# Attention and a mixture of experts on one core: sums kept in PSUM, low parts and softmax scaling between engines, reused w2 parts

## The chip, the cores and the metric

The kernel runs on one core of a Trainium2 chip. A core has TensorE (PE in the profile, with its weight loads as PEld), VectorE (DVE), ScalarE (ACT), GpSimd (POOL) and SyncE (SP, which here only issues DMAs). The metric is the device time of one execution in microseconds (us); lower is better.

## The reference

```python
def _attn_ref(q, k, v, n_global, n_local):            # 4 batches, 8 heads, 768 positions, head size 64
    scores = matmul(q, k^T) / sqrt(D)
    keep = (pos_k < n_global) | ((rel >= 0) & (rel < n_local))       # 8 and 96 here
    scores = where(keep, scores - slopes[h] * dist, -1e9)
    a = exp(scores - max(scores)); a = a / (sum(a) + 1e-9)
    return matmul(a, v)

def _moe_ref(x, domain_probs, w1, w2):                # x: 3072 x 512, 4 experts, 1024 hidden columns
    p = domain_probs / (domain_probs.sum(-1, keepdims=True) + 1e-9)
    for e in range(E):
        h = maximum(x @ w1[e], 0)
        out += p[:, e:e+1] * (h @ w2[e])
    return out
```

The attention's output, heads side by side, is the x of the mixture of experts. All is float32.

## The kernel before

**Precision.** A float32 matrix is split into a high part (a cast to fp32r, on ScalarE) and a low part (the float32 minus that cast). A product is three fp32r matmuls: high by high, low by high, high by low. Every operand of a matmul thus costs a cast and a subtraction; who does the subtraction is a choice between VectorE and GpSimd.

**Fewer products.** Each 2 x 2 block product of the experts is computed with seven block products in place of eight (a Winograd scheme). The weights enter as the sums A11, A12, S3, A22, S2, S1, S4 (`PAIRS1`, `PAIRS2` pack them in pairs), the activations as B11, B21, T3, T4, T2, T1, B22. For w1 the sums are made by `make_pair` in batch 0, written to DRAM by `keep`, and read back in batches 1 to 3. For w2, batch 0 uses plain block products on the raw halves, batch 1 uses the scheme and makes and keeps the sums, batches 2 and 3 read them.

**Units and chunks.** A batch is 16 units (4 experts x 4 groups of 256 hidden columns). `first(i)` is the w1 side of unit i: seven steps, each one product of six 128x384 matmuls. It uses three PSUM tiles: two called y and one z. A step's result is copied out by ScalarE (`part`), or added to such a copy on VectorE (`add`, into the SBUF tile h) and then multiplied by the mixture weight with a maximum against zero in one scalar_tensor_tensor (`weighed`). Two units make a chunk. `second(c)` is the w2 side of chunk c: in batch 0 sixteen steps, later fourteen, of six matmuls each. `hidden(k)` makes the operands of its k-th product: a block sum on VectorE where there is one, the cast on ScalarE, the low part. `collect` adds the PSUM result to the accumulators (`sums_lo` and `third` in the profile).

**Order.** The main loop emits a step of `first`, then a step of `second` for an older chunk (which may start `LAG` steps after its h is complete), and in between steps of the next batch's attention. At a batch's end `blocks` builds the seven operands from x, and six steps of `second` run alone (`ALONE`). In the start and for the first steps the written order is kept (`Ordered.on`); after that a scheduler orders each engine's queue by its own model of costs, and each queue is then executed in order.

**Attention.** `flow` is a pipeline over tiles of 128 queries. In one call a new tile gets its scores, the next older its exponentials, the one after that is scaled by the reciprocal of its sum, the oldest are transposed and weighed (`softmax`, `turn`, `weigh`). `prepare` transposes, splits and spreads queries and keys of a pair of heads in halves of 384 positions; `qd`, the spread query half, has one buffer.

**Buffers.** Weight pairs of w1 have three tiles (`w1p`), those of w2 four (`w2p`, two generations of two). A kept pair is written to DRAM by a DMA on GpSimd's queue as soon as it is made.

The profile gives nearly every instruction the line 42, that of the helper that records it, so rows are told apart by their tiles. Tile `hs` or `third` with reader `h` is an operand of `second`.

Of the kernel before, what the change touches and what calls it, by code (L numbers as in the profile page):

```python
# [185 lines left out]
def attn_moe_kernel(ctx: ExitStack, tc, q, k, v, n_global, n_local, domain_probs, w1, w2, out):  # L186
# [89 lines left out]
    class Pools:  # L276


        def __init__(self, stack, name, st, kd, qd, nat, natv, pb, pT, ps, pt, px):
            def sbuf(part, bufs):  # L280
# [142 lines left out]
    def softmax(A, new, old):  # L423
# [12 lines left out]
        for j in range(2):  # L436
            if new:
                ve.tensor_tensor_reduce(
                    new["pb"][:, j, pcol], ps[:, j, cols], nbias[:, 2 * pr + j, bcol],
                    1.0, 3.0e38, ALU.add, ALU.min, nmax[:, j : j + 1],  # L440
                )
                ac.activation(
                    new["pb"][:, j, pcol], new["pb"][:, j, pcol], AF.Exp, bias=nmax[:, j : j + 1], scale=-1.0,
                    accum_out=new["zsum"][:, j : j + 1],
                )
            if old:
                if j == 0:
                    ve.tensor_scalar_add(zsum, zsum, 1e-9)
                else:
                    ve.reciprocal(zsum, zsum)  # L450
        if old:
            for j in range(2):
                ve.tensor_scalar_mul(pb[:, j, old["pcol"]], pb[:, j, old["pcol"]], zsum[:, j : j + 1])

# [32 lines left out]
    def attention(b, A, early=False):  # L487
# [30 lines left out]
        def prepare(nat, got):  # L518
# [5 lines left out]
            prepare_k(A, nat["k", 0], 0, got)  # L524
            yield 1
            yield 1
            prepare_k(A, nat["k", 1], 1, got)
            yield 1
            nat["vg"] = windows(A, nat["v"])
            yield 1  # L530
            prepare_q(A, nat["q", 1], 1, got)
            yield 1
# [75 lines left out]
    def blocks(b, A, ks=(0, 1), low=po):  # L608
# [18 lines left out]
        yield 1  # L627
        split("B21", b21, low)
        ve.tensor_sub(b12, b22, b12)
# [30 lines left out]
    def split_pair(dst, src):  # L660
        ac.copy(dst[:, 0], src)
        po.tensor_tensor(dst[:, 1], src, f32(dst[:, 0]), op=ALU.subtract)

    def make_pair(dst, pair, q, sums):

        s2, s1 = sums[:, 0], sums[:, 1]
        if pair == ("A11", "A12"):
            po.tensor_add(s1, q[:, 0, 1], q[:, 1, 1])
            po.tensor_sub(s2, s1, q[:, 0, 0])
            split_pair(dst, q[:, :, 0])  # L670
            return
# [5 lines left out]
        if "S4" in pair:  # L677
            po.tensor_sub(q[:, 1, 0], q[:, 1, 0], s2)
        if pair == ("S3", "A22"):
            split_pair(dst, q[:, :, 1])  # L680
            return
        for n, a in enumerate(pair):
            k, m = {"S3": (0, 1), "S4": (1, 0), "A22": (1, 1)}[a]
            split_pair(dst[:, :, n : n + 1], q[:, k : k + 1, m])

    def keep(key, dst, shape):
        kept[key] = dp.tile(shape, F32R, name="kept_" + "_".join(str(n) for n in key))
        po.dma_start(f32(kept[key]), f32(dst))

# [6 lines left out]
    def pair_w1(j):  # L696
# [15 lines left out]
        make_pair(dst.rearrange("p s n (a f) -> p s n a f", a=2), PAIRS1[n], q, sums)  # L712
        keep((1, e, g, n), dst, shape)

# [20 lines left out]
    def next_w2():  # L735
# [6 lines left out]
        for u in range(2):  # L742
            _, e, g = units[2 * c + u]
            shape = [P, 2, 1 if b > 0 and n == 3 else 2, F4]
            dst = wts2[(c, n, u)] = w2p.tile(shape, F32R, name="w2p")
            if b == 0:
                split_pair(dst, raws2[(c, n, u)])
            elif b == 1:
                q = raws2[(c, u)].rearrange("p n (m f) -> p n m f", m=2)
                make_pair(dst, PAIRS2[n], q, sums2[(c, u)])  # L750
                keep((2, e, g, n), dst, shape)
            else:
                sy.dma_start(f32(dst), f32(kept[(2, e, g, n)]))

# [18 lines left out]
    def first(i):  # L773
# [7 lines left out]
        def product(dst, a, x, start=True):  # L781
            j, n = PLACE1[a]
            w = wts1[4 * i + j]
            m = 0
            for kt in range(2):
# [16 lines left out]

        def add(n, pm, other):
            ve.tensor_add(h[n], pm[:, :HALF], other)
            weighed(n, h[n])

# [5 lines left out]
        product(w, "A12", "B21")  # L812
        add("11", w, m1)
        yield
# [7 lines left out]
        product(y, "S3", "T3", start=False)  # L822
        add("22", y, other)
        yield
        product(z, "S4", "B22", start=False)
        add("12", z, part)
        yield
# [11 lines left out]
    def hidden(k):  # L839
# [12 lines left out]
        else:  # L852
            name = SCHEME[n][1]
            eng = ve if name in ("T4", "T1") else po
            if name == "T3":
# [30 lines left out]
    def multiply(pm, c, a, x, m, start, stop):  # L886

        n, u = a
        k = 0
        for kt in range(2):  # L890
# [22 lines left out]
    def second(c):  # L913
# [29 lines left out]
        for n, (a, _) in enumerate(SCHEME):  # L943
# [10 lines left out]
            if last:  # L954

                for eng, to, other in FINAL[n]:
                    eng.tensor_add(slot(b, to), slot(b, to), slot(b, other))
                if n == 5:
# [7 lines left out]
    with ExitStack() as start_stack:  # L966
        A = Pools(start_stack, "start", st=1, kd=2, qd=1, nat=2, natv=3, pb=4, pT=4, ps=3, pt=4, px=1)
        half = iter(())
# [25 lines left out]
    ps_mm = main.enter_context(tc.tile_pool(name="ps_mm", bufs=2, space=PSUM))  # L994
    A = Pools(main, "att", st=1, kd=1, qd=1, nat=3, natv=1, pb=2, pT=3, ps=1, pt=2, px=0)

    LAG, ALONE = 3, 6
    per = 7 * PER  # L1000
    count, span = NPAIR * (6 + NQT) + 5, per - 9
    firsts = (s for i in range(len(units)) for s in first(i))
    seconds = [second(c) for c in range(NCH)]
    xblocks = blocks(0, A, (1,))
    Ordered.on = True
# [4 lines left out]
    def step_second():  # L1010

        nonlocal chunk
        while chunk < NCH and state["done"] >= min(14 * (chunk + 1) + LAG, 7 * len(units)):
            if next(seconds[chunk], 0) is None:
                return True
            chunk += 1
# [84 lines left out]
```

## Time and profile before

| what | value |
|---|---|
| median of 2 runs | 1383.81 us (1383.67 to 1383.95) |
| the profiled execution | 1372.88 us, its span 1371.1 us |
| mean granted TensorE clock | 0.954 |
| PE busy | 1210.3 us (88%), 7201 matmuls |
| DVE busy | 988.5 us (72%), 1919 instructions |
| POOL busy | 664.6 us (48%), 624 instructions |
| ACT busy | 588.5 us (43%), 1271 instructions |
| DMA | 287.28 MB, mean 210 GB/s |

Busy time is the time in which an engine executed something. A stretch of the profile is given in us from the span's start. In a row of instructions the last part, after the second bar, is the idle time of the engine just before them and what ended it. In a row of waits the numbers are us in total, times, and the longest.

### The profile page before, as it was taken

What the parts mean: (1) busy time and instruction counts of PE and PEld (TensorE: products, weight loads), DVE (VectorE), ACT (ScalarE), POOL (GpSimd) and SP (SyncE); (2) the same over time, 40 slices, a digit from 0 to 9 for tenths busy, and PEclk for the clock granted to TensorE, in tenths of its full rate; (3) what the DMA queues carried; (4) which work ended last, traced back from release to release, by engine and by line L of the source; (5) the groups of instructions that cost most, each with busy time, mean ns of one, the idle gap of its engine ahead of it and who ended that gap; (6) DMA issues with size and microseconds to landing.
All of it is one profiled execution on the core that took longest, in us unless ns stands there. A gap on an engine that the chain in (4) does not pass through costs nothing.

```text
span 1371.1 us, 20747 instructions
## 1 busy us (share of the span) xinstructions
PE 1210.3 (88%) x7201; PEld 1148.8 (84%) x7201; DVE 988.5 (72%) x1919; ACT 588.5 (43%) x1271; POOL 664.6 (48%) x624
## 2 busy tenths in 40 slices
PE   6778899999979878879897788989999899999986
PEld 4657889999979778868786688989999799999985
DVE  7767777676766577867788796767787884666665
ACT  4745555455433444435343345444443325322322
POOL 5356666666753275566768742222232523333243
PEclk9989999999999988989998999999999999999999
DMA  7428766666455775757855767868776577777753
GB/s 146 140 71 236 222 193 191 184 210 209 150 165 179 221 227 188 237 195 246 250 200 168 238 195 242 267 201 262 238 253 209 200 250 253 263 256 257 251 202 115
DMA packets 188879, 287.28 MB, mean 210 GB/s; under 512 B 89856, under 2 KB 118624, under 8 KB 188768
## 3 DMA queue, kind: packets, MB, share of 16 engines
q1 hardware_dynamic: 168896, 220.87, 53.0%
q0 software_dynamic: 16384, 58.73, 11.3%
q10 hardware_dynamic: 3488, 6.29, 1.3%
q8 instruction: 59, 0.97, 0.3%
q14 instruction: 52, 0.43, 0.1%
HBM read 197.18 MB, written 65.06 MB: 191 GB/s over the span
## 4 chain that ended last, share of the span: by engine, by line
PE 54%; DVE 18%; DMA 11%; POOL 9%; issue 5%; ACT 4%; SPq 0%; ACTq 0%; DVEq 0%; POOLq 0%
PE pm L42 24%; PE y L42 16%; PE z L42 7%; DVE h L42 7%; PE pt L42 4%; DMA qd<-st_q 4%; POOL hs L42 3%; PE ps L42 3%; DVE pb L42 2%; POOL w2p L42 2%; DMA raw<-in_moe_w_dram 2%; DVE sums_lo L42 2%; DVE zsum L42 1%; DMA w2p<-kept 1%; ACT pb L42 1%
## 5 line engine op out<-in xcount | busy, mean ns | idle before, releaser
L42 PE MATMUL pm<-hs,w2p 128*128 128x384 f32 x2544 | 536.4, 346 | 63.1 <-DVE sums_lo L42 27.4
L42 PEld LDWEIGHTS pm<-hs,w2p 128*128 128x128 f32 x2544 | 459.4, 194 | 81.1 <-issue 17.7
L42 POOL TENSOR_TENSOR hs<-h,hs 128x768 fp32r<-128x768 f32 x120 | 225.6, 1881 | 409.0 <-ACT hs L42 372.8
L42 PE MATMUL y<-xT,w1p 128*128 128x384 f32 x1152 | 252.3, 353 | 23.9 <-DVE h L42 12.9
L42 ACT CAST hs<-h 128x768 fp32r<-128x768 f32 x190 | 158.6, 835 | 214.3 <-PE pm L42 185.7
L42 PEld LDWEIGHTS y<-xT,w1p 128*128 128x128 f32 x1152 | 209.4, 197 | 29.8 <-DVE h L42 14.5
L42 PE MATMUL y<-xB,w1p 128*128 128x384 f32 x768 | 164.8, 347 | 5.3 <-POOL w1p L42 2.5
L42 DVE SCALAR_TENSOR_TENSOR h<-h,mix 128x384 f32<-128x384 f32 x192 | 164.6, 857 | 3.9
L42 DVE TENSOR_TENSOR sums_lo<-pm,sums_lo 128x384 f32<-128x384 f32 x224 | 122.2, 550 | 52.4 <-PE pm L42 51.6
L42 DVE TENSOR_TENSOR h<-h,h 128x768 f32<-128x768 f32 x96 | 103.7, 1081 | 65.6 <-POOL hs L42 65.5
L42 PEld LDWEIGHTS y<-xB,w1p 128*128 128x128 f32 x768 | 135.4, 193 | 9.4 <-POOL w1p L42 3.1
L42 ACT ACTIVATE pb<-pb,nmax 128x256 f32<-128x256 f32 (+1 forms) x192 | 93.3, 487 | 110.3 <-DVE nmax L42 101.5
L42 DVE TENSOR_TENSOR h<-y,part 128x384 f32<-128x384 f32 x128 | 70.7, 552 | 96.0 <-POOL hs L42 43.7
L42 ACT COPY part<-y 128x384 f32<-128x384 f32 x128 | 61.3, 479 | 116.4 <-PE y L42 109.0
L42 DVE TENSOR_SCALAR pb<-pb,zsum 128x256 f32<-128x256 f32 (+1 forms) x192 | 102.3, 568 | 2.9
L42 DVE CUSTOM_DVE_ANT_0 pb<-ps,nbias 128x256 f32<-128x256 f32 (+1 forms) x192 | 71.9, 394 | 38.5 <-PE ps L42 34.6
L42 DVE TENSOR_TENSOR hs<-h,hs 128x768 fp32r<-128x768 f32 x70 | 87.0, 1242 | 13.2 <-ACT hs L42 11.7
L42 DVE TENSOR_TENSOR third<-pm,third 128x384 f32<-128x384 f32 x126 | 68.4, 550 | 32.2 <-PE pm L42 32.1
L42 PE MATMUL z<-xB,w1p 128*128 128x384 f32 x384 | 82.6, 349 | 0.0
L42 PE MATMUL z<-xT,w1p 128*128 128x384 f32 x384 | 81.2, 344 | 1.1 <-ACT xT L42 1.1
L42 PE MATMUL ps<-kd,qd 128*128 128x256 f32 x288 | 54.8, 307 | 28.8 <-DMA qd<-st_q 25.2
L42 POOL TENSOR_TENSOR w2p<-raw,w2p 128x512 fp32r<-128x512 f32 (+1 forms) x48 | 56.2, 1177 | 45.7 <-ACT w2p L42 45.2
(121 smaller groups left out, 1646.5 us busy)
## 6 DMA issues: line engine op xcount, KB each, us to landing
w1p<-kept SPq DMA_DIRECT2D x144, 512.0 KB, 4.5
w2p<-kept SPq DMA_DIRECT2D x96, 512.0 KB, 5.1
kept<-w1p POOLq DMA_DIRECT2D x48, 512.0 KB, 3.7
kept<-w2p POOLq DMA_DIRECT2D x48, 512.0 KB, 4.0
qd<-st_q SPq DMA_DIRECT2D x96, 192.0 KB, 5.1
raw<-in_moe_w_dram SPq DMA_DIRECT2D x32, 512.0 KB, 5.7
w1p<-kept SPq DMA_DIRECT2D x48, 256.0 KB, 3.2
half<-in_moe_w_dram SPq DMA_DIRECT2D x32, 256.0 KB, 3.1
```

The lines of the kernel that those rows point to most:

```text
L42: ins = fn(*args, **kwargs)
```

## The change

- In `first`, the sums of "11", "22" and "12" are written to PSUM (to the bank of "11" for "22", in place for the others) and `weighed` reads them there.
- In `hidden`, in batch 1 all low parts but that of "11" are made by VectorE; in batches 2 and 3 all but those of "11" and "22". Before, VectorE made two of seven. Two low parts of `blocks`, and all the last batch's final sums, go to VectorE too.
- In the attention of batches 1 to 3 ScalarE multiplies the exponentials by the reciprocal; in all batches ScalarE adds the 1e-9.
- Of w2, batch 0 keeps A11, A12 and A22, and batch 1 reads them; it makes S3, S2, S1 and S4.
- `keep` no longer writes at once on GpSimd's queue: the write is noted, and issued on SP's queue when the first product that uses the pair is emitted.
- The second query half is prepared three preparation steps earlier, and `LAG` is 4 in place of 3, one more for the first chunk.

```diff
...
                 )
             if old:
                 if j == 0:
-                    ve.tensor_scalar_add(zsum, zsum, 1e-9)
+                    ac.activation(zsum, zsum, AF.Copy, bias=1e-9)
                 else:
                     ve.reciprocal(zsum, zsum)
         if old:
             for j in range(2):
-                ve.tensor_scalar_mul(pb[:, j, old["pcol"]], pb[:, j, old["pcol"]], zsum[:, j : j + 1])
+                p = pb[:, j, old["pcol"]]
+                if A.scale == "vector":
+                    ve.tensor_scalar_mul(p, p, zsum[:, j : j + 1])
+                else:
+                    ac.activation(p, p, AF.Copy, scale=zsum[:, j : j + 1])
 
     def turn(A, tile_):
 
...
             yield 1
             prepare_k(A, nat["k", 0], 0, got)
             yield 1
+            prepare_q(A, nat["q", 1], 1, got)
             yield 1
             prepare_k(A, nat["k", 1], 1, got)
             yield 1
             nat["vg"] = windows(A, nat["v"])
             yield 1
-            prepare_q(A, nat["q", 1], 1, got)
             yield 1
 
         def prepare_all(pr):
...
 
         split("B11", b11, ve)
         yield 1
-        split("B21", b21, low)
+        split("B21", b21, ve)
         ve.tensor_sub(b12, b22, b12)
         yield 1
         ve.tensor_add(b11, b12, b11)
...
         ac.copy(dst[:, 0], src)
         po.tensor_tensor(dst[:, 1], src, f32(dst[:, 0]), op=ALU.subtract)
 
+    def make_sums(q, sums):
+        po.tensor_add(sums[:, 1], q[:, 0, 1], q[:, 1, 1])
+        po.tensor_sub(sums[:, 0], sums[:, 1], q[:, 0, 0])
+
     def make_pair(dst, pair, q, sums):
 
-        s2, s1 = sums[:, 0], sums[:, 1]
         if pair == ("A11", "A12"):
-            po.tensor_add(s1, q[:, 0, 1], q[:, 1, 1])
-            po.tensor_sub(s2, s1, q[:, 0, 0])
+            make_sums(q, sums)
             split_pair(dst, q[:, :, 0])
             return
         if pair == ("S2", "S1"):
...
         if "S3" in pair:
             po.tensor_sub(q[:, 0, 1], q[:, 0, 0], q[:, 0, 1])
         if "S4" in pair:
-            po.tensor_sub(q[:, 1, 0], q[:, 1, 0], s2)
-        if pair == ("S3", "A22"):
-            split_pair(dst, q[:, :, 1])
-            return
+            po.tensor_sub(q[:, 1, 0], q[:, 1, 0], sums[:, 0])
         for n, a in enumerate(pair):
             k, m = {"S3": (0, 1), "S4": (1, 0), "A22": (1, 1)}[a]
             split_pair(dst[:, :, n : n + 1], q[:, k : k + 1, m])
 
-    def keep(key, dst, shape):
-        kept[key] = dp.tile(shape, F32R, name="kept_" + "_".join(str(n) for n in key))
-        po.dma_start(f32(kept[key]), f32(dst))
+
+    waiting = {}
+
+    def keep(pair):
+        for key, src, shape in waiting.pop(pair, ()):
+            kept[key] = dp.tile(shape, F32R, name="kept_" + "_".join(str(n) for n in key))
+            sy.dma_start(f32(kept[key]), f32(src))
 
     def load_w1(i):
         if i < PER:
...
         q = raws1[i].rearrange("p (n a) (m f) -> p n m a f", n=2, m=2)
 
         make_pair(dst.rearrange("p s n (a f) -> p s n a f", a=2), PAIRS1[n], q, sums)
-        keep((1, e, g, n), dst, shape)
+        waiting[(1, j)] = [((1, e, g, n), dst, shape)]
 
 
     seq2 = [(c, n) for c in range(NCH) for n in (range(2) if c < CPB else range(4))]
...
             shape = [P, 2, 1 if b > 0 and n == 3 else 2, F4]
             dst = wts2[(c, n, u)] = w2p.tile(shape, F32R, name="w2p")
             if b == 0:
+
                 split_pair(dst, raws2[(c, n, u)])
-            elif b == 1:
-                q = raws2[(c, u)].rearrange("p n (m f) -> p n m f", m=2)
-                make_pair(dst, PAIRS2[n], q, sums2[(c, u)])
-                keep((2, e, g, n), dst, shape)
-            else:
-                sy.dma_start(f32(dst), f32(kept[(2, e, g, n)]))
+                waiting.setdefault((2, c, n), []).append(
+                    ((2, e, g, n), dst, shape) if n == 0 else ((2, e, g, 4), dst[:, :, 1:], [P, 2, 1, F4])
+                )
+                continue
+            one = dst[:, :, :1]
+            if n == 0 or b > 1:
+                sy.dma_start(f32(one if n == 1 else dst), f32(kept[(2, e, g, n)]))
+            if n == 1:
+                sy.dma_start(f32(dst[:, :, 1:]), f32(kept[(2, e, g, 4)]))
+            if b > 1:
+                continue
+            q, sums = raws2[(c, u)].rearrange("p n (m f) -> p n m f", m=2), sums2[(c, u)]
+            if n == 0:
+                make_sums(q, sums)
+                continue
+            make_pair(one if n == 1 else dst, (("S3",), ("S2", "S1"), ("S4",))[n - 1], q, sums)
+            waiting.setdefault((2, c, n), []).append(
+                ((2, e, g, n), one if n == 1 else dst, [P, 2, 2 if n == 2 else 1, F4])
+            )
 
         if made2[0] < len(seq2):
             c1, n1 = seq2[made2[0]]
...
         def product(dst, a, x, start=True):
             j, n = PLACE1[a]
             w = wts1[4 * i + j]
+            keep((1, 4 * i + j))
             m = 0
             for kt in range(2):
                 for wi, xi in ((0, 0), (1, 0), (0, 1)):
...
             ac.copy(dst, src[:, :HALF])
             return dst
 
-        def add(n, pm, other):
-            ve.tensor_add(h[n], pm[:, :HALF], other)
-            weighed(n, h[n])
+        def add(n, to, pm, other):
+            ve.tensor_add(to[:, :HALF], pm[:, :HALF], other)
+            weighed(n, to[:, :HALF])
 
         y = ps_h.tile([P, 512], F32, name=f"y{i % 2}")
         product(y, "A11", "B11")
...
         yield
         w = ps_h.tile([P, 512], F32, name=f"y{1 - i % 2}")
         product(w, "A12", "B21")
-        add("11", w, m1)
+        add("11", w, w, m1)
         yield
         product(y, "S2", "T2", start=False)
         part = copy(y)
...
         other = copy(z)
         yield
         product(y, "S3", "T3", start=False)
-        add("22", y, other)
+        add("22", w, y, other)
         yield
         product(z, "S4", "B22", start=False)
-        add("12", z, part)
+        add("12", z, z, part)
         yield
         product(y, "A22", "T4", start=False)
         weighed("21", y[:, :HALF])
...
             src, eng = h[PLAIN[n]], ve
         else:
             name = SCHEME[n][1]
-            eng = ve if name in ("T4", "T1") else po
+            eng = po if name == "11" or name == "22" and c >= 2 * CPB else ve
             if name == "T3":
                 ve.tensor_sub(h["12"], h["22"], h["12"])
             elif name == "T4":
...
     def multiply(pm, c, a, x, m, start, stop):
 
         n, u = a
+        keep((2, c, n))
         k = 0
         for kt in range(2):
             w = wts2[(c, n, kt)]
...
             if last:
 
                 for eng, to, other in FINAL[n]:
+                    eng = ve if b == B - 1 else eng
                     eng.tensor_add(slot(b, to), slot(b, to), slot(b, other))
                 if n == 5:
                     yield from output(b, 0, 1, 3)
...
     mp = main.enter_context(tc.tile_pool(name="mp", bufs=3))
     Ordered.on = True
     with ExitStack() as start_stack:
-        A = Pools(start_stack, "start", st=1, kd=2, qd=1, nat=2, natv=3, pb=4, pT=4, ps=3, pt=4, px=1)
+        A = Pools(start_stack, "start", st=1, kd=2, qd=1, nat=2, natv=3, pb=4, pT=4, ps=3, pt=4, px=1, scale="vector")
         half = iter(())
         mix = mixture(A)
         for n, _ in enumerate(attention(0, A, early=True)):
...
     tp2 = main.enter_context(tc.tile_pool(name="third", bufs=1))
     ps_h = main.enter_context(tc.tile_pool(name="ps_h", bufs=1, space=PSUM))
     ps_mm = main.enter_context(tc.tile_pool(name="ps_mm", bufs=2, space=PSUM))
-    A = Pools(main, "att", st=1, kd=1, qd=1, nat=3, natv=1, pb=2, pT=3, ps=1, pt=2, px=0)
-
-
-
-    LAG, ALONE = 3, 6
+    A = Pools(main, "att", st=1, kd=1, qd=1, nat=3, natv=1, pb=2, pT=3, ps=1, pt=2, px=0, scale="scalar")
+
+
+
+    LAG, ALONE = 4, 6
     per = 7 * PER
     count, span = NPAIR * (6 + NQT) + 5, per - 9
     firsts = (s for i in range(len(units)) for s in first(i))
     seconds = [second(c) for c in range(NCH)]
-    xblocks = blocks(0, A, (1,))
+    xblocks = blocks(0, A, (1,), ve)
     Ordered.on = True
     next(xblocks)
     next(xblocks)
...
     def step_second():
 
         nonlocal chunk
-        while chunk < NCH and state["done"] >= min(14 * (chunk + 1) + LAG, 7 * len(units)):
+        while chunk < NCH and state["done"] >= min(14 * (chunk + 1) + LAG + (chunk == 0), 7 * len(units)):
             if next(seconds[chunk], 0) is None:
                 return True
             chunk += 1
```

The pools of the start are made with `scale="vector"`, those of the other batches with `scale="scalar"`.

More of the change, by code (lines that the diff above doesn't have):

```diff
@@ L276, in attn_moe_kernel, with __init__ @@
     class Pools:
-        def __init__(self, stack, name, st, kd, qd, nat, natv, pb, pT, ps, pt, px):
+        def __init__(self, stack, name, st, kd, qd, nat, natv, pb, pT, ps, pt, px, scale):
+            self.scale = scale
             def sbuf(part, bufs):
```

## The prediction

> **What bounds the kernel now.** I first read the busy shares and the forty slices of the page, then cut the span where a batch's first w1 product starts (75, 401, 760 and 1065 us) and where the last w1 product ends (1322 us), and asked for the busy time of each stretch.
>
> ```profile
> PE 1210.3 (88%) x7201; PEld 1148.8 (84%) x7201; DVE 988.5 (72%) x1919; ACT 588.5 (43%) x1271; POOL 664.6 (48%) x624
> 75.00:401.00 326.00, 292.84 (x1799) 279.63 (x1799) 234.19 (x434) 163.24 (x370) 217.70 (x245) 0.97 0.60 187
> 401.00:760.00 359.00, 303.57 (x1737) 289.64 (x1738) 262.78 (x463) 153.29 (x330) 206.84 (x200) 0.90 0.66 212
> 760.00:1065.00 305.00, 280.33 (x1720) 267.16 (x1719) 231.21 (x476) 130.51 (x285) 103.62 (x73) 0.97 0.74 233
> 1065.00:1322.00 257.00, 247.32 (x1401) 243.11 (x1400) 174.29 (x277) 84.10 (x132) 86.68 (x46) 0.99 0.71 244
> 1322.00:1371.00 49.00, 33.80 (x173) 28.86 (x171) 28.65 (x41) 11.76 (x16) 17.56 (x9) 0.95 0.38 136
> 1150.00:1300.00 150.00, 149.43 (x861) 148.85 (x860) 97.16 (x167) 48.07 (x75) 47.87 (x26) 1.00 0.75 257
> ```
>
> The columns are stretch, length, then busy us (and count) of PE, PEld, DVE, ACT and POOL, the granted TensorE clock, DMA share and GB/s. The share of 88% on PE is an average over unlike stages. The last row is what a PE-bound stage looks like: 149.4 of 150 us busy, 861 matmuls, 0.174 us each, clock 1.00. Batches 1 and 2 (rows 3 and 4) run the same matmuls (1737 and 1720), yet batch 1 needs 359 us and batch 2 only 305. What differs is POOL: 207 us against 104, since batch 1 also builds the w2 combinations. DVE is busier too, 263 against 231 us for the same list of instructions, and the clock is 0.90 against 0.97. So in batch 1 PE is not the bound. What ends its waits, and what DVE spends, is in the next rows, all of 401 to 760 us.
>
> ```profile
> PE pm L42 <- DVE sums_lo L42: 19.4, 7, 5.5
> PE y L42 <- DVE h L42: 12.9, 4, 5.7
> DVE h L42 <- POOL hs L42: 28.8, 10, 8.0
> L42 DVE SCALAR_TENSOR_TENSOR h<-h,mix 128x384 f32<-128x384 f32 x48 | 49.5, 1032 | 0.9
> L42 DVE SCALAR_TENSOR_TENSOR h<-y,mix 128x384 f32<-128x384 f32 x16 | 8.7, 547 | 0.6 <-PE y L42 0.6
> L42 DVE TENSOR_TENSOR h<-h,h 128x768 f32<-128x768 f32 x27 | 34.4, 1276 | 5.6 <-POOL hs L42 5.6
> L42 DVE TENSOR_SCALAR pb<-pb,zsum 128x256 f32<-128x256 f32 (+1 forms) x48 | 33.8, 740 | 0.7
> L42 DVE TENSOR_SCALAR zsum<-zsum 128x2 f32<-128x2 f32 x24 | 12.6, 525 | 8.7 <-ACT pb L42 8.7
> L42 DVE TENSOR_TENSOR hs<-h,hs 128x768 fp32r<-128x768 f32 x14 | 19.1, 1364 | 0.3 <-ACT hs L42 0.2
> L42 POOL TENSOR_TENSOR hs<-h,hs 128x768 fp32r<-128x768 f32 x34 | 64.1, 1887 | 48.0 <-ACT hs L42 47.8
> L42 POOL DMA_DIRECT2D kept<-w2p x54 | 30.2, 560 | 7.1 <-POOL w2p L42 4.2 <-issue 2.4 <-PE y L42 0.3
> L42 POOL TENSOR_TENSOR w2p<-raw,w2p 128x512 fp32r<-128x512 f32 (+1 forms) x40 | 48.1, 1210 | 42.1 <-ACT w2p L42 41.7
> ```
>
> PE waits mostly for DVE, and DVE waits 28.8 us for POOL's low parts. The two scalar_tensor_tensor rows do the same arithmetic on the same 128x384: from PSUM it takes 547 ns, from SBUF 1032. The scaling (740 ns) and even an add on two columns (525 ns) are far above their size. One stretch shows why.
>
> ```profile
> 602.76 0.36 DVE L42 TENSOR_SCALAR pb<-pb,zsum 128x256 f32<-128x256 f32 x1
> 602.91 0.57 POOL L42 DMA_DIRECT2D kept<-w2p  x1
> 603.04 6.31 DVE L42 SCALAR_TENSOR_TENSOR h<-h,mix 128x384 f32<-128x384 f32 x1
> 603.51 1.30 POOL L42 TENSOR_TENSOR w2p<-raw,w2p 128x512 fp32r<-128x512 f32 x1
> 604.76 1.81 POOL L42 TENSOR_TENSOR hs<-h,hs 128x768 fp32r<-128x768 f32 x1
> 607.12 1.81 POOL L42 TENSOR_TENSOR hs<-h,hs 128x768 fp32r<-128x768 f32 x1
> 609.97 2.26 PE L42 MATMUL pm<-hs,w2p 128*128 128x384 f32 x6 [4.32 <-DVE sums_lo L42]
> ```
>
> An instruction of half a microsecond stands for 6.31 us while POOL works without a gap, and PE then idles 4.32 us for the accumulation queued behind it. A DVE instruction on SBUF operands is slowed by a busy POOL. The PSUM form is not: 547 ns beside the busiest POOL.
>
> **The change, part by part.** All terms are us of the profiled execution (1372.88, span 1371.1).
>
> *PSUM outputs.* Three adds per unit now write PSUM and the weighing reads PSUM. No row has a DVE write to PSUM. The nearest, a DVE read from it, differs from the SBUF form by 0.14 us at the least (687 against 547, below), so I bound the add's cost by 0.14 either way, 7 per batch, and take zero. The weighing goes from 1032 to 547: batch 1 gains 48 x 0.485 = 23.3. The other batches:
>
> ```profile
> L42 DVE SCALAR_TENSOR_TENSOR h<-h,mix 128x384 f32<-128x384 f32 x48 | 48.3, 1007 | 1.3
> L42 DVE SCALAR_TENSOR_TENSOR h<-h,mix 128x384 f32<-128x384 f32 x46 | 33.9, 737 | 0.8
> L42 DVE SCALAR_TENSOR_TENSOR h<-h,mix 128x384 f32<-128x384 f32 x51 | 35.0, 687 | 0.9
> ```
>
> Batches 0, 2, 3 in order: 22, 9 and 7. [...]
>
> The add's sum now stays in a bank: "22" is put where "11" was, two products before the next unit starts in that bank. DVE must be under two products (4.2 us) late. The bank of "21" already allows it only one, and with it PE waits 12.9 us on `h` in batch 1, so I cost the new wait at nothing; without that cover each microsecond of lateness is 16 us per batch.
>
> *Softmax on ScalarE.* DVE loses 33.8 and 12.6 in batch 1. ACT gains 48 instructions. The nearest rows are these, of the whole run:
>
> ```profile
> L42 ACT ACTIVATE pb<-pb,nmax 128x256 f32<-128x256 f32 x160 | 80.6, 505 | 87.0 <-DVE nmax L42 81.1 <-DVE zsum L42 5.7
> L42 ACT CAST w1p<-raw 128x256 fp32r<-128x256 f32 x48 | 18.2, 405 | 23.4 <-PE y L42 12.1 <-POOL raw L42 8.4 <-POOL w1p L42 1.1
> L42 ACT ACTIVATION_READ_ACCUMULATOR pb<-pb,nmax 128x1 f32 x192 | 36.1, 188 | 0.0
> ```
>
> Bounds 0.405 and 0.505; with a per-partition scale I take the second, 24 us, plus 24 x 0.19 = 5 for the small add. ACT goes from 153 to some 180 of 300 us, beside everything. Behind the new ACT instructions stand the evacuations and casts; the transposes that use the scaled tile come a whole softmax step later, which covers half a microsecond. [...]
>
> *Low parts.* In batch 1 four of seven move from POOL to DVE per chunk, 32 in all; three in batches 2 and 3, 24 each. Bounds: 0.95 undisturbed (the 954 below, same size) and 1.364 as now. POOL will still be some 40% busy; I take 1.15, so +36.8 in batch 1. A moved low part also waits for its ACT cast; the accumulations and weighings queue behind it. The 14 already there waited 0.3 in total. In return DVE no longer waits for POOL before overwriting a block, -28.8, and its block sums fall from 1276 to batch 2's 1068, 27 x 0.21 = -5.6.
>
> ```profile
> L42 DVE TENSOR_TENSOR h<-h,h 128x768 f32<-128x768 f32 x31 | 33.1, 1068 | 21.8 <-POOL hs L42 21.8
> L42 DVE TENSOR_TENSOR h<-h,h 128x768 f32<-128x768 f32 x38 | 36.3, 954 | 38.2 <-POOL hs L42 38.1
> L42 DVE TENSOR_SCALAR pb<-pb,zsum 128x256 f32<-128x256 f32 (+1 forms) x48 | 23.8, 530 | 0.6
> PE ps L42 <- DMA qd<-st_q: 25.2, 9, 4.5
> L42 POOL TENSOR_TENSOR w1p<-sums,w1p 128x512 fp32r<-128x512 f32 x16 | 20.9, 1306 | 14.9 <-ACT w1p L42 14.8
> L42 ACT CAST w1p<-sums 128x512 fp32r<-128x512 f32 x16 | 9.9, 616 | 23.0 <-issue 13.1 <-POOL sums L42 4.4 <-POOL raw L42 2.1
> kept<-w1p POOLq DMA_DIRECT2D x48, 512.0 KB, 3.7
> w2p<-kept SPq DMA_DIRECT2D x96, 512.0 KB, 5.1
> ```
>
> *Reuse of w2, and the kept writes on SP.* POOL loses in batch 1 the 32 low parts (60), its DMA issues (30) and the A11, A12 and A22 splits (some 35): from 207 to about 80. The reused parts come back by DMAs issued two generations ahead; 5.1 us each, hidden as in batch 2, which reads all weights so at DMA share 0.74. The 128 kept writes now stand in SP's queue ahead of q, k, w1 and qd transfers, and are issued only when TensorE first uses the pair. A pair is rewritten three or more products before its use; a product of six matmuls alternates with six of w2, 12 x 0.174 = 2.1, so 6.2 us; the landing of 3.7 lies beside the pair's own second product. I cost it at nothing; the second rival prices it.
>
> *Query halves, LAG, last sums.* The second query half is transposed three preparation steps earlier. Its buffer is single, so the transfer still waits for the third tile's scores, and only the transposing and splitting leave the 25.2 us wait: I take a third, 8 over three batches, inside the sums below. One more step of lag gives low parts 2 us more; no cost, since PE's list is unchanged.
>
> **The sum.** *Batch 1:* DVE's queue -23.3 - 33.8 - 12.6 + 36.8 - 5.6 - 28.8 = -67, which would give 292. PE cannot go much below batch 2's 280 busy, and I let batch 1 reach batch 2's present 305: -54 (bounds -20, if a third of the relief arrives, and -80, PE nearly dense). *Batch 2:* DVE -9 - 24 - 8 + 25 = -16, with half of 22 of POOL waits and a share of qd, but PE idles only 25 of 305: -10 (0 to -22). *Batch 0:* weighing, scaling and issue relief all fall on a stage with 33 idle: -15 (0 to -30). *Batch 3 and tail:* PE has 10 idle of 257; the tail idles 15 of 49 and its lows go from 1.89 to 0.95: -6 (+4 to -15). Start: 0. Together -85: 1372.9 - 85 = 1288. The median of the runs, 1383.81, is 0.8% above the profiled 1372.88; on that scale 1298.
>
> **Rivals.**
> 1. *DVE becomes the bound.* It takes over 80 instructions. If low parts stay at 1.364 and each waits for its ACT cast as long as it does now for POOL, batch 1 gets back 7 + 29 of its 67 and loses some more in PE's coupling: -20, other batches -12 in all: 1341, or 1351 on the scale of the median. For it: DVE is already 73% busy in batch 1, its one cover an idle POOL. Against it: batch 2 runs at 76% with PE at 92%. 0.17.
> 2. *Slower: the kept writes hold their pairs.* A w1 pair cannot be refilled before its write has landed. If SP is stuck behind another wait when TensorE takes up a pair, the write comes late, cast and low part after it, and PE waits. The chain is 3.7 landing + 0.6 cast + 1.3 low part = 5.6 of 6.2 us; so it bites from 0.6 us of SP lateness. If each of batch 0's 64 pairs costs 2 us, +128: 1372.9 - 85 + 128 = 1416, 1427 on the median's scale. For it: SP's queue is in order. Against: many pairs have four or five products, and SP only issues. 0.05.
> 3. *Within 2%.* The scheduler reorders around the new costs; what DVE gains is lost to qd, ACT and clock waits, and about 15 remain: 1358, 1369. 0.08.
>
> **How the numbers follow.** The forecast holds 0.70. Its own bounds are -42 to -130 with terms that don't all end together; the 80% range runs from 1255 (-128 before scaling) to 1350, which takes in most of the first rival. A change under 2% (1356 to 1411) is what I take a measurement of this kernel as unable to tell from none: faster 0.87, same 0.08, slower 0.05.
>
> **What would show it.** After: `h` weighing entirely from PSUM near 550 ns; the wait of DVE for POOL's low parts gone in batch 1; POOL near 80 us there; low parts on DVE near 1.1 us; batch 1's clock at 0.96 or more and its length near 300. Wrong if DVE is over 90% busy in batch 1, if PE's waits name `kept` DMAs or ACT's `w1p`, or if PE waits at a unit's first product for "22".

## The result

The changed kernel takes 1285.81 us (median of 1281.94 and 1289.68) against 1383.81 before: ratio 0.929, 95% interval 0.917 to 0.941. Run again later beside the other versions, it took 1281.99 against 1372.26: 0.935, interval 0.930 to 0.940. The median of one and the same kernel differs by about 1% between sessions (for the kernel before 1383.81, 1369.98, 1369.29 and 1372.26 us), so what follows compares ratios to the kernel before of the same session. The profiled execution took 1281.94 (span 1280.1) against 1372.88.

First the stages of these two profiled executions, again as busy time of stretches (length, then busy us and counts of PE, PEld, DVE, ACT, POOL, the clock, DMA share, GB/s). This time the cuts are where a batch's first w1 matmul stands by count (672 to a batch). By that count batch 2 ends at 1081 before, not at the 1065 of the prediction, so the rows of before are given for these cuts too; the kernel before, then the changed one:

```profile
80.00:392.00 312.00, 285.49 (x1750) 273.43 (x1750) 228.15 (x424) 158.18 (x359) 210.89 (x242) 0.97 0.62 192
392.00:755.00 363.00, 303.95 (x1742) 290.05 (x1741) 262.20 (x462) 153.66 (x331) 212.00 (x202) 0.90 0.65 208
755.00:1081.00 326.00, 294.29 (x1781) 280.24 (x1780) 250.02 (x496) 138.87 (x296) 112.55 (x79) 0.96 0.73 231
1081.00:1324.00 243.00, 237.93 (x1364) 234.31 (x1365) 162.48 (x265) 77.88 (x123) 79.40 (x42) 1.00 0.73 250
```

```profile
85.00:391.00 306.00, 288.11 (x1753) 273.77 (x1752) 166.50 (x356) 177.84 (x431) 172.78 (x179) 0.98 0.74 237
391.00:692.00 301.00, 279.13 (x1731) 268.12 (x1729) 204.99 (x411) 163.78 (x388) 104.29 (x103) 0.97 0.81 252
692.00:988.00 296.00, 282.53 (x1779) 271.23 (x1778) 225.29 (x448) 158.91 (x364) 57.94 (x41) 1.00 0.81 253
988.00:1234.00 246.00, 239.97 (x1369) 234.64 (x1368) 186.00 (x296) 80.05 (x126) 35.27 (x19) 1.00 0.73 248
1234.00:1280.00 46.00, 32.01 (x169) 26.83 (x168) 31.77 (x46) 11.81 (x17) 5.52 (x3) 0.98 0.45 150
```

Batch 1 is 62 us shorter, batch 2 30, batch 0 6; batch 3 is 3 longer, the start 5 longer. The stages of a second profiled execution of the changed kernel lie within about 2 us of these. Of batch 1's 62 us, TensorE's idle time gave 37 (59 to 22) and its busy time for the same matmuls 25 (304 to 279), while the granted clock went from 0.90 to 0.97; no run here separates the clock from the idle time. Batch 1 now runs like batch 2, with POOL at a half. The rows that answer to those of before, from 391 to 692 us of the changed kernel (groups, then waits):

```profile
L42 DVE SCALAR_TENSOR_TENSOR h<-y,mix 128x384 f32<-128x384 f32 x47 | 25.9, 552 | 1.2 <-PE y L42 0.5
L42 DVE TENSOR_TENSOR y<-y,part 128x384 f32<-128x384 f32 x32 | 17.9, 560 | 15.4 <-PE y L42 11.6 <-PE pm L42 1.8 <-issue 1.0
L42 DVE TENSOR_TENSOR hs<-h,hs 128x768 fp32r<-128x768 f32 x39 | 42.8, 1098 | 21.7 <-ACT hs L42 21.7
L42 DVE TENSOR_TENSOR h<-h,h 128x768 f32<-128x768 f32 x26 | 28.1, 1081 | 20.9 <-POOL hs L42 20.7
L42 ACT ACTIVATE pb<-pb,zsum 128x256 f32<-128x256 f32 (+1 forms) x48 | 21.2, 487 | 15.2 <-DVE zsum L42 15.2
L42 ACT ACTIVATE zsum<-zsum 128x2 f32<-128x2 f32 x24 | 4.9, 204 | 0.5
```

```profile
PE y L42 <- ACT part L42: 9.9, 3, 7.3
PE ps L42 <- DVE nmax L42: 5.0, 1, 5.0
PE pm L42 <- DMA w2p<-kept: 3.6, 4, 1.4
```

The add costs the same into PSUM (560 ns) as it did into SBUF (552), the weighing 552, scaling on ScalarE 487. PE's 19.4 us of waits for the accumulations and 12.9 for h no longer stand in the list.

### The profile page after: what moved, and what is told of

Its sections match the earlier page's. It is cut to its first block, busy times and chain, and to the rows that moved or that the text cites. A ratio compares the mean times of both kernels' runs of the same rounds, so it can differ in the third digit from the quotient of the medians.

```text
span 1280.1 us, 20773 instructions
## 1 busy us (share of the span) xinstructions
PE 1179.6 (92%) x7201; PEld 1117.9 (87%) x7201; DVE 871.8 (68%) x1768; ACT 642.9 (50%) x1495; POOL 405.1 (32%) x391
## 4 chain that ended last, share of the span: by engine, by line
PE 47%; DMA 11%; DVE 4%; ACT 2%; POOL 2%; issue 2%; SPq 1%; ACTq 0%; DVEq 0%; POOLq 0%
PE pm L42 23%; PE y L42 13%; DMA w2p<-kept 7%; PE z L42 7%; PE pt L42 3%; DMA out_dram<-hs 2%; PE ps L42 1%; ACT hs L42 1%; DVE h L42 1%; DMA raw<-in_moe_w_dram 1%; POOL hs L42 1%; SPq L42 1%; DVE third L42 1%; DVE hs L42 1%; DMA kept<-w2p 1%
## 5 line engine op out<-in xcount | busy, mean ns | idle before, releaser
L42 PE MATMUL pm<-hs,w2p 128*128 128x384 f32 x2544 | 518.3, 338 | 27.1 <-DMA w2p<-kept 13.8
L42 PEld LDWEIGHTS pm<-hs,w2p 128*128 128x128 f32 x2544 | 445.0, 188 | 43.5 <-issue 13.9
L42 PEld LDWEIGHTS y<-xT,w1p 128*128 128x128 f32 x1152 | 201.6, 191 | 28.8 <-ACT part L42 13.5
L42 POOL TENSOR_TENSOR hs<-h,hs 128x768 fp32r<-128x768 f32 x40 | 74.1, 1853 | 418.9 <-ACT hs L42 351.2
L42 DVE TENSOR_TENSOR hs<-h,hs 128x768 fp32r<-128x768 f32 x150 | 158.9, 1060 | 59.5 <-ACT hs L42 58.7
L42 DVE SCALAR_TENSOR_TENSOR h<-y,mix 128x384 f32<-128x384 f32 x192 | 105.8, 552 | 20.0 <-POOL hs L42 15.5
L42 DVE TENSOR_TENSOR y<-y,part 128x384 f32<-128x384 f32 x128 | 71.7, 561 | 58.3 <-PE y L42 43.0
L42 POOL TENSOR_TENSOR w1p<-raw,w1p 128x512 fp32r<-128x512 f32 (+1 forms) x64 | 58.9, 934 | 81.4 <-ACT w1p L42 77.9
L42 ACT ACTIVATE pb<-pb,zsum 128x256 f32<-128x256 f32 (+1 forms) x144 | 64.6, 487 | 30.7 <-DVE zsum L42 30.7
L42 PE MATMUL pt<-ident,pb 128*128 128x128 f32 x352 | 58.7, 281 | 14.9 <-DVE pb L42 13.1
```

Of the source, the lines that this page charges most:

```text
L42: ins = fn(*args, **kwargs)
```

## The experiments

I split the change into five parts, ran four of them alone, and ran the changed kernel with each of the five taken out. *Theory 1*, the prediction's: the gain is VectorE's time, given back because its instructions are fewer and not stretched by GpSimd. *Theory 2*: GpSimd's queue was the brake, and what it delays, TensorE and VectorE wait for. The two do not exclude each other: a loaded GpSimd may stand behind both VectorE's 28.8 us of waits for its low parts and the weighings of 1042 ns from SBUF, 547 from PSUM, in batch 1 before.

### One part alone

Sums in PSUM:

```diff
-        def add(n, pm, other):
-            ve.tensor_add(h[n], pm[:, :HALF], other)
-            weighed(n, h[n])
+        def add(n, to, pm, other):
+            ve.tensor_add(to[:, :HALF], pm[:, :HALF], other)
+            weighed(n, to[:, :HALF])
```

> The kernel before with one part of the change: the sums of 11, 22 and 12 stay in PSUM. If VectorE's time is what was gained (theory 1), the weighing falls from 857 to about 550 ns and VectorE loses some 60 us of busy time, half of it in batch 1; PE's waits for h and the sums shrink, and the time falls by 25 to 35 us, to about 1353. If GpSimd's queue was the brake (theory 2), VectorE goes on waiting for GpSimd's low parts and the time falls by under 10. If TensorE's new waits for the held banks bite, PE's waits at y name DVE and the time does not fall.

Measured: 1356.12 against 1369.98, ratio 0.988 (0.981 to 0.996). Faster by 14, half of what theory 1 gave it, though the weighing now reads PSUM, where it takes 552 ns in the changed kernel for 1042 before. Its batch 1, and the scaling there:

```profile
389.00:739.00 350.00, 294.49 (x1743) 280.73 (x1742) 255.66 (x465) 153.40 (x331) 211.24 (x202) 0.93 0.69 216
L42 DVE TENSOR_SCALAR pb<-pb,zsum 128x256 f32<-128x256 f32 (+1 forms) x48 | 38.7, 836 | 0.7
```

The weighing alone was worth 23 us of VectorE's time in this stage, but its busy time fell by 7 (262 to 256): other instructions took longer, the scaling among them, 836 ns instead of 740.

Scaling on ScalarE:

```diff
-                    ve.tensor_scalar_add(zsum, zsum, 1e-9)
+                    ac.activation(zsum, zsum, AF.Copy, bias=1e-9)
...
+                    ac.activation(p, p, AF.Copy, scale=zsum[:, j : j + 1])
```

> The kernel before with one part of the change: ScalarE scales the exponentials in batches 1 to 3 and adds the 1e-9. Theory 1: VectorE loses about 110 us of busy time, a third of it in batch 1, and the time falls by 25 to 40 us, to about 1350. Theory 2: under 10, since GpSimd's list is the same.

Measured: 1367.43, ratio 0.998 (0.994 to 1.001): no gain clear of the noise. Its page's first line of busy times, its batch 1, and VectorE's wait there for GpSimd's low parts:

```profile
PE 1210.7 (88%) x7201; PEld 1146.9 (84%) x7201; DVE 882.7 (64%) x1679; ACT 652.4 (48%) x1511; POOL 666.2 (49%) x624
407.00:753.00 346.00, 295.90 (x1739) 281.68 (x1738) 221.30 (x390) 171.58 (x402) 213.98 (x202) 0.93 0.69 218
DVE h L42 <- POOL hs L42: 54.3, 19, 6.0
```

VectorE lost 106 us of busy time and the kernel did not move. In batch 1 its busy time fell by 41 (262 to 221), but its wait for GpSimd rose from 28.8 to 54.3, so more than half of what VectorE saved there it spent waiting. The rest did pay: the stage was 17 shorter. But the start was 5 longer, batch 0 10 (312 to 322) and batch 2 four, which takes the 17 back; in batch 0 TensorE's wait for qd rose from 8.8 to 15.7. So the run speaks against theory 1's 25 to 40 us for the whole kernel, and only in part against it in batch 1.

Low parts on VectorE:

```diff
-            eng = ve if name in ("T4", "T1") else po
+            eng = po if name == "11" or name == "22" and c >= 2 * CPB else ve
```

> The kernel before with one part of the change: 80 low parts of the w2 operands, and a few others, go from GpSimd to VectorE. Theory 1: VectorE's relief by waits (29 us in batch 1) and its added work (37 there) cancel, so the time stays within 12 us of 1384, and VectorE is over 80% busy in batch 1. Theory 2: GpSimd loses 150 us, and the time falls by 40 or more.

Measured: 1326.66, ratio 0.968 (0.960 to 0.975). Theory 2's 40 us, from adding 80 instructions to VectorE. First the weighing from SBUF in the kernel before, from 392 to 755 us, then this run's batch 1:

```profile
L42 DVE SCALAR_TENSOR_TENSOR h<-h,mix 128x384 f32<-128x384 f32 x47 | 49.0, 1042 | 0.9
```

```profile
390.00:718.00 328.00, 289.36 (x1735) 276.55 (x1734) 255.36 (x487) 152.13 (x330) 162.78 (x173) 0.95 0.73 232
L42 DVE TENSOR_TENSOR hs<-h,hs 128x768 fp32r<-128x768 f32 x40 | 48.8, 1219 | 4.9 <-ACT hs L42 4.6
L42 DVE SCALAR_TENSOR_TENSOR h<-h,mix 128x384 f32<-128x384 f32 x47 | 35.5, 755 | 0.8
L42 DVE TENSOR_SCALAR pb<-pb,zsum 128x256 f32<-128x256 f32 (+1 forms) x48 | 21.0, 469 | 0.5
DVE h L42 <- POOL hs L42: 7.3, 3, 3.5
```

VectorE does 26 low parts more and is busy 7 us less (255 against 262): the weighing went from 1042 over this stage (1032 in the prediction's cut) to 755, the scaling from 740 to 469, and the wait for GpSimd from 28.8 to 7.3. Both theories' effects are there, and this run does not say how much each gave.

Reuse of w2, kept writes on SP:

```diff
-        po.dma_start(f32(kept[key]), f32(dst))
+            sy.dma_start(f32(kept[key]), f32(src))
...
+            if n == 0 or b > 1:
+                sy.dma_start(f32(one if n == 1 else dst), f32(kept[(2, e, g, n)]))
```

> The kernel before with one part of the change: batch 1 reads A11, A12 and A22 of w2 back, and the kept writes are issued on SP. VectorE's list of instructions is the same. Theory 1: since GpSimd is less busy by some 65 to 100 us in batches 0 and 1, VectorE's instructions on SBUF get shorter there (weighing in batch 1 from 1032 to 800 or less), and the time falls by 15 to 30 us. Theory 2: VectorE's instructions keep their length, but the waits for GpSimd go, and the time falls by 40 or more. If the kept writes hold up their pairs, PE or ACT waits name kept DMAs and the time rises.

Measured: 1332.36, ratio 0.969 (0.962 to 0.976). Its batch 1:

```profile
386.00:728.00 342.00, 296.20 (x1744) 280.08 (x1743) 232.67 (x467) 144.18 (x319) 163.26 (x132) 0.93 0.73 226
L42 DVE SCALAR_TENSOR_TENSOR h<-h,mix 128x384 f32<-128x384 f32 x48 | 39.7, 826 | 0.9
L42 DVE TENSOR_SCALAR pb<-pb,zsum 128x256 f32<-128x256 f32 (+1 forms) x48 | 21.8, 488 | 0.8
DVE h L42 <- POOL hs L42: 39.8, 15, 5.3
```

VectorE's list is unchanged, GpSimd does less (163 us for 212). The gain of 38 is near theory 2's 40, but it did not come the way theory 2 said: VectorE's wait for GpSimd rose from 28.8 to 39.8. What fell is VectorE's busy time, by 30 (262 to 233), with the weighing at 826 and the scaling at 488 ns, as in theory 1. So two quite different ways to relieve GpSimd are each worth some 3%, one with VectorE's wait for it shorter and one with that wait longer. The four parts alone sum to 7.8%; the whole is 6.5 to 7.1%.

In batch 1 the two effects can be added up. In us, the length of the stage, VectorE's busy time, its wait for GpSimd's low parts, and what is left:

| version | stage | busy | wait | rest |
|---|---|---|---|---|
| before | 363 | 262 | 29 | 72 |
| sums in PSUM | 350 | 256 | 25 | 69 |
| scaling on ScalarE | 346 | 221 | 54 | 70 |
| low parts on VectorE | 328 | 255 | 7 | 65 |
| reuse of w2 | 342 | 233 | 40 | 70 |
| changed | 301 | 205 | 21 | 75 |

Each part alone shortened the stage by about what it took from busy time and wait together (13 for 10, 17 for 15, 35 for 28, 21 for 18). This holds for batch 1 of these versions; in batch 0 VectorE is busy 62 us less in the changed kernel, and the stage is 6 shorter.

### One part taken out

Each of these is the changed kernel with the lines above put back.

> The changed kernel with the scaling of the exponentials and the 1e-9 put back on VectorE. Alone this part gave 3 us. If the parts simply add (theory A: what counts is GpSimd's load), undoing it costs about 3 us, 1287 or so. If it is the low parts on VectorE that make VectorE's time scarce (theory B), it costs 20 us or more: VectorE gets 60 to 80 us of busy time back, batch 1 is over 80% VectorE, and PE waits for h and the sums.

Measured: 1279.35, ratio 0.933 (0.926 to 0.941). The same as the changed kernel (0.935). In batch 1 VectorE is busy 20 us longer (225 for 205) and the stage is 302 us for 301: with TensorE busy 279 of 301 us, VectorE's time hardly counts there.

> The changed kernel with the sums of 11, 22 and 12 put back into SBUF. Alone this part gave 14 us. Theory A: undoing it costs about 14 us, or less, since with a quieter GpSimd the weighing from SBUF takes 600 to 650 ns. Theory B: 25 us or more.

Measured: 1309.73, ratio 0.956 (0.948 to 0.964): it costs 2.1%, some 28 us, twice what it gave alone. This is the only part whose interval lies clear of that of the changed kernel (0.930 to 0.940).

> The changed kernel with the low parts put back on GpSimd. Alone this part gave 43 us. Theory A: undoing it costs 35 to 45 us, with VectorE's waits for GpSimd's low parts back. If the other parts already took away what made GpSimd late (theory B), 20 us or less.

Measured: 1294.27, ratio 0.944 (0.936 to 0.952): 12 us. VectorE's wait for GpSimd in batch 1 is back, 51 us for 21, but VectorE is busy 16 us less there (189 for 205) and the stage is only 7 longer.

> The changed kernel with all w2 sums made again in batch 1 and the kept writes back on GpSimd's queue. Alone this part gave 38 us. Theory A: undoing it costs 30 to 40 us, most of it in batch 1. Theory B: 20 us or less, since GpSimd without the low parts has room.

Measured: 1291.15, ratio 0.943 (0.935 to 0.951): 9 to 11 us. The low parts and the weights gave 43 and 38 alone and 12 and some 10 last: I read this as two parts that take load off the same engine, so that little is left for the second; no run has these two alone together. Both intervals overlap that of the changed kernel, so the sizes are rough.

Where the sums cost this can be read by stages. With them in SBUF the profiled execution is 22 to 23 us longer: batch 0 by 5, batch 2 by 8 to 10, the last by 9 to 10, and batch 1, for which the prediction had the most, not at all. The last batch's stretch and PE's wait for h in it, with the sums in SBUF, and then in the second run of the changed kernel:

```profile
1001.00:1257.00 256.00, 242.76 (x1369) 235.98 (x1368) 190.99 (x296) 79.90 (x126) 35.17 (x19) 0.99 0.72 239
PE y L42 <- DVE h L42: 6.7, 6, 1.2
```

```profile
988.00:1235.00 247.00, 240.26 (x1368) 234.60 (x1368) 185.87 (x295) 79.89 (x126) 35.26 (x19) 1.00 0.74 247
PE y L42 <- DVE h L42: 0.2, 1, 0.2
```

GpSimd is hardly busy there (35 us) and VectorE differs by 5 us of busy time. What differs more is that TensorE waits for its y bank: 6.7 us here, 12.8 in the whole run against 0.9. I read it as low parts of a microsecond standing in VectorE's queue ahead of the read that frees the bank; that was not tried by itself. These waits are about half of the loss; the rest is not settled.

### The order, and a ghost of the low parts

The changed kernel with no edit, as reference:

> The changed kernel itself, so that the four undone versions have their reference beside the same kernel before: ratio 0.93 to 0.94, 1275 to 1287 us. Undoing the scaling gave 1279, so if scaling on ScalarE is worth anything in company, this one lies below 1275.

Measured: 1281.99, ratio 0.935 (0.930 to 0.940).

```diff
-            prepare_q(A, nat["q", 1], 1, got)
             yield 1
             prepare_k(A, nat["k", 1], 1, got)
...
+            prepare_q(A, nat["q", 1], 1, got)
...
-    LAG, ALONE = 4, 6
+    LAG, ALONE = 3, 6
```

> The changed kernel with the second query half prepared late again and LAG 3. The prediction priced the query part at 8 us and LAG at nothing: 1287 or so, with PE's wait for qd back at 8 to 12 us. If the order carries more of the whole than that (the four single parts without it still wait 12 to 30 us for qd), undoing it costs 15 us or more.

(The first chunk's extra step of lag is taken out as well.) Measured: 1287.96, ratio 0.940 (0.934 to 0.947). Six us, near the eight priced, but the intervals overlap. By stages batches 1 and 2 are some 5 and 8 longer and batch 3 is 4 shorter. PE's wait for qd, 1.3 us with the change, is back at 13.5.

Then the question of why GpSimd's load costs: its results are late, or VectorE is slowed beside it. The kernel before with low parts on VectorE, and on GpSimd work of about the same time that nobody reads:

```diff
+        if k >= plain and eng is ve and SCHEME[n][1] not in ("T4", "T1"):
+            for kt, lo, hi in ((0, 0, 192), (0, 192, 384), (1, 0, 192)):
+                part = f32(dst[:, 0, kt, lo:hi])
+                po.tensor_tensor(ghost[:, : hi - lo], part, part, op=ALU.subtract)
```

> The kernel before with the low parts on VectorE, and beside each moved low part three GpSimd subtractions of the same operand into a tile that nobody reads (576 of 768 elements, about the time of the moved low part): GpSimd's load is as before, but nobody waits for those results. If the 43 us of the low parts came from the waits for GpSimd's results, it stays near 1327, and VectorE's waits for GpSimd stay near 45 us. If they came from GpSimd's load (its other work late, and VectorE's SBUF instructions slowed beside it), it goes back to 1360 or more, with the weighing from SBUF near 1000 ns again in batch 1.

Measured: 1343.07, ratio 0.979 (0.973 to 0.984). Between the two. Its batch 1:

```profile
394.00:732.00 338.00, 289.95 (x1731) 276.10 (x1730) 255.68 (x486) 152.56 (x330) 215.63 (x249) 0.94 0.71 224
L42 POOL TENSOR_TENSOR ghost<-hs 128x192 f32<-128x192 f32 x78 | 57.2, 733 | 23.0 <-ACT hs L42 19.5
L42 DVE SCALAR_TENSOR_TENSOR h<-h,mix 128x384 f32<-128x384 f32 x47 | 35.0, 746 | 0.8
DVE h L42 <- POOL hs L42: 11.7, 4, 4.2
```

GpSimd is as busy as before (216 against 212) and 25 of batch 1's 35 us stay gained (363, 338, 328). So by the ratios about two thirds of the low parts' gain stay although GpSimd is no less busy; the intervals leave from two fifths to all. Whether they come from nobody waiting for GpSimd's results (11.7 us of wait for 28.8) or from VectorE's shorter instructions this run can't tell, since the weighing did not go back to 1000 ns: it stayed at 746 with GpSimd busy 216 of 338 us. Nor is the lost third in VectorE's instructions: its busy time is the same in both runs (255.7 and 255.4). Where it is was not found. What the run does show is that GpSimd's busy share alone does not stretch the weighing: it took 746 ns with GpSimd busy for 64% of the batch, and 1042 before with 58%. The ghost's pieces take 0.73 us, a low part 1.89, and they read one operand in place of two; which of these matters was not tried.

Last, a version from these results: scaling back on VectorE, and in batch 3, where GpSimd is 14% busy, low parts back on GpSimd.

```diff
+            if c >= 3 * CPB:
+                eng = ve if name in ("T4", "T1") else po
+            else:
+                eng = po if name == "11" or name == "22" and c >= 2 * CPB else ve
```

> A version put together from the results: the changed kernel with the scaling and the 1e-9 back on VectorE, and in the last batch, where GpSimd is 14% busy, the low parts back on GpSimd. From the stages of the runs so far: the undone scaling costs nothing (1279), the last batch falls from 246 to 242: about 1275. If the scheduler's order eats this, 1279 to 1285.

Measured: 1281.26, ratio 0.936 (0.931 to 0.941). The changed kernel's time; the last batch stayed at 246 and no gain came of it.

## Why the prediction was right, and where not

The time was forecast at 1298 and came at 1286; on the profiled scale -85 was forecast and -91 came. By stages: batch 1 -54 forecast, -62 measured, length near 300, clock 0.97, all as said. Batch 0 -15, -6. Batch 3 and the tail -6, +2. The start 0, +5: the first w1 matmul stands at 84 to 85 us with the 1e-9 on ScalarE (the changed kernel, scaling alone, the reuse of w2 taken out) and at 80 before, with it on VectorE, a price I had as nothing. Batch 2 -10, -30; here the step that failed is "PE idles only 25 of 305", taken from a cut that ended batch 2 sixteen us early. By count it was 326 long; PE's idle time there fell by 18 and its busy time by 12, with the clock from 0.96 to 1.00.

The total was right with wrong prices on its parts. The sum ran along VectorE's queue. Its prices for single instructions held: weighing 550, scaling 0.5 on ScalarE, low parts 1.15 forecast and 1.10 measured, no loss from a PSUM output, no wait for the bank of "22". The floor held too: TensorE is busy 279 of batch 1's 301 us, where 280 of 305 was put. Even VectorE's -67 in batch 1 came, as -65 of busy time and wait together (291 to 226). But this is in part luck: busy time fell by 57 where the terms give 38.5, the wait by 8 where they give 28.8, and the two misses of some 20 us cancel. What failed is the pricing by parts: each part was given its own instructions on VectorE, and what it does to GpSimd's queue, and so to VectorE's waits and to the length of its other instructions, was left out.

- *Scaling*, with its small add priced at -46 in batch 1 and -32 in batch 2, gave 3 us alone, with an interval that includes no gain, and nothing in company. In batch 1 alone more than half of the relief became a wait for GpSimd; the 17 us left were lost in other stages.
- *Low parts*, priced at +37 - 29 - 6 = +2 in batch 1, gave 35 there alone and 43 in all; in company 12. The term that was mis-sized is the price of GpSimd's load. I took it as the 28.8 us that VectorE idled and 6 of block sums; but with 26 low parts more VectorE was busy 7 us less.
- *Weights*, priced at zero with some 65 us of GpSimd relief in batch 1 (issues and splits) counted as cover only, gave 38 alone and some 10 in company. GpSimd's own queue was left out of the sum.
- *PSUM sums*, -23, -22, -9 and -7 of VectorE's time, 61 in all, gave 14 alone and 28 last: half or less. Alone, 16 of batch 1's 23 went into other instructions that took longer, the scaling (836 ns for 740) among them.

Rival 1, VectorE as the bound, did not come: VectorE's busy share of batch 1 fell to 68% (205 of 301). One of its two conditions came in large part: the low parts waited 21.7 us for their casts, where it put 29. The other did not: they took 1.10 us and not 1.364. In the kernel before VectorE was 73% busy with most of TensorE's waits in its name. Those name the last link; behind it stood GpSimd, whose relief shortened VectorE's instructions in both runs that gave it (the weighing 755 and 826 ns for 1042), and VectorE's wait in one of them (7.3 us for 28.8).

Rival 2 happened in small. Two rows of waits of the changed kernel show the kept writes holding their pairs in batch 0, and its TensorE waiting for w1 (3.3 us before):

```profile
ACT w1p L42 <- DMA kept<-w1p: 23.3, 11, 5.7
PE y L42 <- POOL w1p L42: 8.4, 9, 2.9
```

With the writes back on GpSimd (and none of w2 in batch 0) the first row shrinks to 2.8 us and batch 0 takes 300 us in place of 306. So in company "at nothing" was some 6 us wrong, and with it much of the -15 of batch 0; alone the same part made batch 0 shorter (306 for 312). Writes issued earlier on SP might give it back; that was not tried. VectorE's wait for GpSimd in batch 1 did not go, as I had said it would: 20.7 us are left, and GpSimd's busy time there is 104 us where I said about 80.

## What to carry to other kernels

A wait is put down to its last link. Before pricing relief for the engine that is named, look at what that engine waits for: shorten it alone, and see whether its wait for another grows, as here from 28.8 to 54.3 us. Busy time and wait belong in one sum, since relief can move from one to the other. Two parts that unload the same queue need not add up: here they gave 43 and 38 us alone, 12 and some 10 last.

When several edits meet, price each along every queue it touches, and not along one; a total can come out right on terms that do not.

## What the runs showed of the hardware

The weighing from PSUM kept a mean of 546 to 554 ns in every batch of the kernel before and of the changed one, with GpSimd busy from 14 to 68% of the batch, and 546 to 549 in batch 1 of four of the other runs; from SBUF its means in the batches of the kernel before ran from 624 to 1042. GpSimd as busy as ever, but in pieces of 0.73 us, left it at 746. An add from PSUM to PSUM took 560 ns against 552 to SBUF.

So the split in the weighing goes with its source, 554 ns at most against up to 1042. The 6.31 us of the prediction's stretch are longer than any one GpSimd instruction there (1.81); the gap between the two low parts there holds one more DMA issue of GpSimd (at 606.52, 0.57 us), which the stretch leaves out. What held the weighing for so long no run shows.

Scaling on ScalarE brought neither a gain nor a loss that shows in the time: ratio 0.998 alone, and 0.933 without it against 0.935 with it. The start was 5 us longer with the 1e-9 on ScalarE. The scaling took 487 ns on ScalarE, against 740 on VectorE in batch 1 before and 469 there with the low parts moved.
